# The last chunk's first MLP layer by 20 products of blocks in place of 22

## The chip, the cores and the metric

The kernel runs on one core of a Trainium2 chip. The metric is the device time of one launch in microseconds. All times below are of this kernel before the change: three timed runs, and one execution taken by the hardware profiler.

## What is computed

The reference has two stages. A recurrence (a delta rule) runs over 768 tokens for 4 batches of 8 heads of dimension 48; its output, 3072 tokens by 384, goes through an MLP with a SiLU:

```
for t in range(S):
    y[t]  = q[t] @ state
    v_old = k_n[t] @ state
    state = state + beta[t] * outer(k_n[t], v[t] - v_old)
x = y as (B*S, H*D)                 # 3072 x 384
h = x @ w_in                        # 384 x 2048
out = (h * sigmoid(h)) @ w_out      # 2048 x 384
```

All of it is in float32.

## The kernel before

**Chunks.** The 768 tokens are six chunks of 128 (c = 0 to 5, `NCH` = 6), and each chunk has two halves of 64 tokens (`hf`). The recurrence of chunk c (`solve(c)`, and the inversion of its triangular blocks beforehand, `invert`) is interleaved with the MLP of the chunk before it. A half's tokens of all four batches are 256 columns (`GT`); a chunk's inputs to the MLP are the two tiles `xTs[c, 0]` and `xTs[c, 1]`, each three blocks of 128 rows by 256 columns.

**One order per engine.** `pin` chains every compute instruction to the one before it on its engine, and `in_line` does so with the DMAs of SyncE. So the order in which the program calls things is the order in which each engine executes them. An instruction that waits holds up everything behind it on its engine.

**MLP in steps.** The MLP is a generator, `pieces`; `run(n)` advances it by n steps. The outer loop over c advances the recurrence by a stage (`go(solving)`) and the MLP by one or two steps in turn. For c = 5 there are eight such passes (n = 0 to 7), with these stages of the recurrence: the first merge (tile py, line 847; evacuated into y), the keys of the first half (ph, line 893; VectorE adds ph into vf, line 898), the second merge (px, line 847; into xi), the inner products and the old state's outputs of the first half (pz, line 905, and pyc, line 973), the update of the state with the new outputs (pu, line 925, with VectorE's addition to state at line 932; pyc, line 986), the copies of the outputs into xT, the keys of the second half (ph and vf again), and the inner products of the second half (pz and pyc again). Meanwhile the MLP steps are those of chunk 4's second layer. A last stage makes the outputs of the second half, and the rest of the MLP then runs to the end.

**First layer, chunks 2 to 5** (`hidden_by_products`, matmuls at line 1168). The weights w_in are three blocks of rows by pairs of column blocks; f counts 16 blocks of 128 columns, two to a pair. With the two halves of the tokens this makes small block products, of which linear combinations save some: 22 products for two units of two pairs each, instead of 24, on sums of weights (tile sums_of_w_in, made once) and sums of inputs (`sum_x`, five subtractions, line 1156). One product is `product(...)`: two matmuls of 128x128 weights by 256 columns into one PSUM bank. A chunk has 44 products in a list `items`; after some of them ScalarE copies the bank into gT (`by_act`, line 600), VectorE adds it to gT (line 1183), or ScalarE applies the Silu (lines 1189 and 1195). Banks of PSUM are handed out in turn: `hu` takes the two banks that the second layer's px and py had, `hx` two others.

**Second layer** (`combine(c, hf)`, matmuls at line 1334). For each half there are seven chains of eight matmuls of 192 columns, into px and py by turns; each chain is two MLP steps. In the middle of some chains VectorE makes sums of gT (`sum_g`, S1 to S4, line 1314) for later chains. Behind chains, ScalarE copies a bank into kept (line 1342), which frees it, and VectorE adds kept to o (line 1345); kept is one buffer. In the middle of the seventh chain of hf = 1 the kernel makes the next chunk's sums of inputs.

Of the kernel before, what the change touches and what calls it, by code (L numbers as in the profile page):

```python
# [10 lines left out]
FP32 = mybir.dt.float32  # L11
U32 = mybir.dt.uint32
ACTF = mybir.ActivationFunctionType
ALU = mybir.AluOpType
# [5 lines left out]
def kernel(  # L20
# [10 lines left out]
    nc = tc.nc  # L31
    B, H, S, D = q.shape
    DM, DFF = moe_w_in.shape
    P = 128
    C = P
    assert S % C == 0 and D == 48 and H == 8 and B == 4 and DM == H * D and DM == 3 * P
    NCH = S // C
# [5 lines left out]
    NKT = DM // P  # L43
    NFF = DFF // P
    HB = B // 2
    HH = HB * H
    GT = B * W
# [9 lines left out]
    banks = ctx.enter_context(tc.tile_pool(name="banks", bufs=1, space=PSUM))  # L57
# [5 lines left out]
    def bank(room, name):  # L63

        tag = room[0]
        room.rotate(-1)
        return pools.get(tag, banks).tile([P, 512], FP32, name=name, tag=tag)
# [12 lines left out]
    def pin(op):  # L80

        engine = op.ins.engine
        if engine in pins:
            behind(op, pins[engine])
        pins[engine] = op
        return op
# [19 lines left out]
    def go(steps, n=1):  # L106
        for _ in range(n):
            next(steps, None)
# [25 lines left out]
    spare_s = wS[:].rearrange("p k f t -> p (k f t)")  # L134
# [464 lines left out]
    def by_act(to, of):  # L599
        return pin(nc.scalar.copy(to, of))  # L600
# [496 lines left out]
    def home(c, hf):  # L1097

        return 1 - hf if c < 2 else hf
# [32 lines left out]
    def w_of(a, j):  # L1132
        return w_in[:, a].rearrange("p (f j t) -> p f j t", j=2, t=P)[:, :, j]
# [14 lines left out]
    def sum_x(c):  # L1148

        early, late = (xTs[c, hf] for hf in range(2))  # L1150
        for to, left, right in (
            (sums_of_x[:, 0], late[:, 0], early[:, 0]), (sums_of_x[:, 1], late[:, 1], sums_of_x[:, 0]),
            (late[:, 0], late[:, 1], late[:, 0]), (sums_of_x[:, 2], early[:, 1], sums_of_x[:, 1]),
            (sums_of_x[:, 3], early[:, 2], late[:, 2]),
        ):
            pin(nc.vector.tensor_tensor(out=to, in0=left, in1=right, op=ALU.subtract))

    def hidden_by_products(c):
# [68 lines left out]
        for n, (to, weights, moving, fs, start, after) in enumerate(items):  # L1227
# [8 lines left out]
                CC.append(rooms[1])  # L1236
            yield

    def store(c, hf, o, n, cols=slice(0, DM), two_queues=False):
        for u in range(HB):  # L1240
            row = (n * HB + u) * S + c * C + hf * W
            issue(out[row : row + W, cols], o[W * u : W * (u + 1), n, cols], two_queues and u == 1)
# [76 lines left out]
    def combine(c, hf):  # L1319

        o = mlp.tile([P, 2, DM], FP32, name="o", bufs=1)
        kept = mlp.tile([P, HM], FP32, name="kept", bufs=1)
        px, py = bank(M, "px"), bank(M, "py")
        left, right = slice(0, HM), slice(HM, DM)
        last = c == NCH - 1 and hf == 1
        order = list(range(NFF // 2)) if c < 2 else [2 * u + i for u in UNITS for i in range(2)]

        def chain(to, a, b, start=False):
            for n, f in enumerate(order):
                if isinstance(a, int):  # L1330
                    at = sums_of_g[:, a, f]
                else:
                    at = gT[:, home(c, hf), f, a[0] * GT + a[1] * C : a[0] * GT + (a[1] + 1) * C]
                pin(nc.tensor.matmul(  # L1334
                    to, lhsT=at, rhs=quarter(f, *b) if isinstance(b, tuple) else sums_of_w[b][:, f],
                    start=start and n == 0, stop=n == NFF // 2 - 1, skip_group_check=True,
                ))
                if n % 4 == 3:
                    yield

        def keep(of):
            pin(nc.scalar.mul(kept[:], of, 0.5))  # L1342

        def add(to, of):
            pin(nc.vector.tensor_tensor(out=to, in0=to, in1=of, op=ALU.add))  # L1345

        def steps(chain, *halfway):
            for n, _ in enumerate(chain):
                if n == 1:
                    break  # L1350
                for what in halfway:
                    if what is sum_x:
                        sum_x(c + 1)
                    else:
                        sum_g(c, *(what if len(what) == 3 else (hf, *what)))
                yield

        first, then, ahead, parts = (), (), (), PARTS
        if c < 2:
            first, parts = ((S1, NG - 1), (S2, NG - 1)), range(NG)  # L1360
        elif hf == 0:
            first, then = (tuple((which, fs) for fs in PARTS) for which in (S1, S2))
        else:
            first = tuple((S2, fs) for fs in PARTS)
        if hf == 1 and c + 1 < NCH:
            ahead = (sum_x,)
        elif hf == 0 and c > 1:
            ahead = tuple((1, S1, fs) for fs in PARTS)
        yield from steps(chain(px[:, left], (0, 0), (0, 0), True), *first)
        yield  # L1370
        yield from steps(chain(px[:, right], (1, 1), 2), *then)
        pin(nc.scalar.mul(o[:, :, left], px[:, 0:DM].rearrange("p (n m) -> p n m", n=2), 0.5))
        yield
        yield from steps(chain(py[:, left], 0, (0, 1), True))
        pin(nc.scalar.mul(o[:, 1, right], py[:, left], 0.5))
        yield
        yield from steps(chain(px[:, left], 1, 1), *((S3, g) for g in parts))
        pin(nc.scalar.mul(o[:, 0, right], px[:, left], 0.5))
        yield
        yield from steps(chain(py[:, right], (1, 0), (1, 0)), *((S4, g) for g in parts))  # L1380
        keep(py[:, right])
        add(o[:, 0, left], kept[:])
        if last:
            store(c, hf, o, 0, left)
        yield
        yield from steps(chain(px[:, left], 0, 0))
        keep(px[:, left])
        add(o[:, 1].rearrange("p (n m) -> p n m", n=2), kept[:].unsqueeze(1).to_broadcast([P, 2, HM]))
        if last:
            store(c, hf, o, 1)  # L1390
        yield
        yield from steps(chain(py[:, left], 1, (1, 1)), *ahead)
        if last:
            pin(nc.vector.scalar_tensor_tensor(
                out=o[:, 0, right], in0=py[:, left], scalar=0.5, in1=o[:, 0, right], op0=ALU.mult, op1=ALU.add
            ))
            store(c, hf, o, 0, right, True)
            yield
            return
        keep(py[:, left])  # L1400
        add(o[:, 0, right], kept[:])
        for n in range(2):
            store(c, hf, o, n)
        yield

    def feed_forward(c):

        if c > 1:
            yield from hidden_by_products(c)
        for hf in range(2):  # L1410
            if c == 1:
                yield from hidden(c, hf)
            yield from combine(c, hf)
# [209 lines left out]
    def run(n=1):  # L1623

        for _ in range(n):
            done[0] += 1
            name = next(needed, None)
            if name is not None:
                until(name)
            go(pieces)  # L1630
            begin_soon()
# [147 lines left out]
    def start(c):  # L1779

        return 2 * (NFF + OUTPUT) + (c - 2) * (ITEMS + 2 * OUTPUT)

    def run_to(at):

        assert done[0] <= at
        run(at - done[0])
# [40 lines left out]
    for c in range(2, NCH):  # L1827
        solving, more = solve(c), c + 1 < NCH
        for n in range(8):
            go(solving)  # L1830
            run((1, 1, 2, 2, 1, 1, 2, 2)[n] if c == 2 else (2, 2, 2, 2, 1, 1, 2, 2)[n])
            if n == 2 and c > 2 and more:
                assert done[0] >= start(c) - OUTPUT - 4
                load_blocks(k, c + 1, G1)
            if n == 3 and c > 2 and more:
                load_blocks(q, c + 1, G0)
            if n > 0:
                go(after, 8)
        go(after, 99)
        go(solving)  # L1840
        run()
        assert next(solving, 0) == 0
        if c == 2:
            pieces = chained(pieces, *(feed_forward(c) for c in range(2, NCH)))
        if not more:
            break
        run(1 if c == 2 else 2)
        step = block_steps(c + 1)
        ready = prepare(c + 1)
        go(ready)  # L1850
        run()
        go(ready)
        go(sums_in)
        go(sums_in)
        linked(load_v, c + 1)
        load_k(c + 2)
        run_to(start(c))
        paced(invert(c + 1, step), 7 if c == 2 else 4)
        after = lengths(c + 2) if c + 2 < NCH else iter(())
        run_to(start(c) + ITEMS + 3)  # L1860
        for g in range(2):
            size(c + 1, g)
        for n in range(3 if c == 2 else 2):
            go(after, 2 - n)
            run()
        go(after, 1)
# [31 lines left out]
```

## Time and profile before

| | |
|---|---|
| median of three runs | 630.88 us (628.24 to 633.61) |
| the profiled execution, its own time | 628.09 us |
| its span, first to last instruction | 626.3 us |
| mean granted clock of TensorE | 0.986 |
| busy: TensorE, VectorE, ScalarE, GpSimd | 610.0, 442.5, 244.4, 82.0 us |

The span is what the trace shows; the time of the execution has 1.8 us around it. A busy time is a sum over instructions of one engine; a row of a timeline gives the start, the length, the engine, the line, the operation, the tiles and the shapes, and in brackets how long the engine had been idle and what ended that. PE is TensorE's matmuls, PEld its weight loads, DVE VectorE, ACT ScalarE, POOL GpSimd.

### The profile page before, as it was taken

Reading aid. Unit: us, or ns where it says so; the run is one execution under the profiler, and the core shown is the slowest. Engines: PE = TensorE matmul, PEld = TensorE weight load, DVE = VectorE, ACT = ScalarE, POOL = GpSimd, SP = SyncE. Lnnn points to the kernel's source line nnn. Section 1 sums busy time; section 2 is a strip of 40 time slices with the busy share of each in tenths; the row PEclk is TensorE's granted clock in tenths of the full one; section 3 lists DMA queues with packets and bytes.
Section 4 is the critical chain, followed back from the end, with each engine's and each line's share of the span. In section 5 each row is a group of like instructions: output and inputs, shape, how many; then the busy total and the mean of one; then the engine's idle time right before and its main releaser. Section 6 shows DMA issues by size and latency. Waiting matters only on the chain.

```text
span 626.3 us, 21887 instructions
## 1 busy us (share of the span) xinstructions
PE 610.0 (97%) x9570; PEld 535.0 (85%) x9570; DVE 442.5 (71%) x946; ACT 244.4 (39%) x554; POOL 82.0 (13%) x83
## 2 busy tenths in 40 slices
PE   7889999999999999999999999999999999999997
PEld 5678788666789988898888998899998899988997
DVE  5855889998889975879977869976868944321332
ACT  3656655251351134443424433423533324434201
POOL 5443631246000010000010000010000010000000
PEclk9859999999999999999999999999999999999999
DMA  7754654164426571245073444084350051010011
GB/s 157 175 119 160 213 137 102 51 170 123 104 48 135 99 146 33 66 88 108 0 157 96 93 105 90 6 151 115 82 121 16 19 94 38 18 27 0 1 26 26
DMA packets 143935, 55.06 MB, mean 88 GB/s; under 512 B 113488, under 2 KB 137296, under 8 KB 143840
## 3 DMA queue, kind: packets, MB, share of 16 engines
q1 hardware_dynamic: 143360, 53.00, 37.8%
q8 instruction: 75, 1.23, 0.8%
q10 hardware_dynamic: 480, 0.67, 0.4%
q14 instruction: 20, 0.16, 0.1%
HBM read 40.99 MB, written 10.49 MB: 82 GB/s over the span
## 4 chain that ended last, share of the span: by engine, by line
PE 93%; DMA 2%; ACT 2%; issue 1%; DVE 1%; SPq 0%; DVEq 0%
PE px L1334 16%; PE phid L1114 13%; PE hu L1168 13%; PE py L1334 12%; PE hx L1168 11%; PE po L1257 7%; PE pa L585 4%; PE pz L905 3%; PE ph L893 2%; PE pyc L986 2%; PE pu L925 2%; PE pyc L973 2%; PE pt L556 1%; PE py L847 1%; PE px L847 1%
## 5 line engine op out<-in xcount | busy, mean ns | idle before, releaser
L1114 PE MATMUL phid<-xT,w_in 128*128 128x256 f32 x384 | 88.9, 385 | 0.0
L1114 PEld LDWEIGHTS phid<-xT,w_in 128*128 128x128 f32 x384 | 71.1, 190 | 10.0 <-issue 0.3
L1334 PE MATMUL py<-w_out,sums_of_g 128*128 128x192 f32 x320 | 57.4, 329 | 0.8 <-issue 0.8
L1334 PE MATMUL px<-sums_of_w,sums_of_g 128*128 128x192 f32 x320 | 57.2, 330 | 0.0
L1334 PEld LDWEIGHTS py<-w_out,sums_of_g 128*128 128x128 f32 x320 | 52.2, 190 | 1.5 <-issue 0.9
L1334 PEld LDWEIGHTS px<-sums_of_w,sums_of_g 128*128 128x128 f32 x320 | 52.1, 190 | 1.0 <-issue 0.5
L688 DVE SCALAR_TENSOR_TENSOR rank<-g,step,x 128x31 f32<-128x31 f32 (+15 forms) x124 | 49.6, 400 | 3.1
L1168 PE MATMUL hx<-xT,w_in 128*128 128x256 f32 x192 | 48.0, 379 | 0.0
L693 DVE TENSOR_TENSOR x<-x,rank 128x31 f32<-128x31 f32 (+15 forms) x124 | 42.5, 342 | 4.4
L1168 PE MATMUL hu<-xT,w_in 128*128 128x256 f32 x192 | 45.4, 379 | 0.0
L1183 DVE TENSOR_TENSOR gT<-gT,hx 128x512 f32<-128x512 f32 x32 | 21.9, 686 | 33.0 <-PE hx L1168 32.3
L1314 DVE TENSOR_TENSOR sums_of_g<-gT 128x512 f32<-128x512 f32 (+2 forms) x44 | 27.5, 662 | 22.6 <-PE py L1334 18.8
L1168 PEld LDWEIGHTS hu<-xT,w_in 128*128 128x128 f32 x192 | 36.5, 190 | 5.0
L1168 PEld LDWEIGHTS hx<-xT,w_in 128*128 128x128 f32 x192 | 36.4, 190 | 4.8
L521 POOL TENSOR_TENSOR vf<-vf,n_slot 128x768 f32<-128x768 f32 x10 | 14.6, 1476 | 189.8 <-DVE sums_of_g L1314 147.3
L1345 DVE TENSOR_TENSOR o<-o,kept 128x192 f32<-128x192 f32 (+1 forms) x29 | 12.4, 426 | 36.3 <-ACT kept L1342 36.3
L600 ACT COPY xT<-pyc 48x128 f32<-48x128 f32 (+2 forms) x120 | 31.2, 260 | 1.6
L600 ACT COPY gT<-hu 128x512 f32<-128x512 f32 x32 | 18.8, 586 | 30.6 <-PE hu L1168 30.6
L932 DVE TENSOR_TENSOR state<-state,pu 48x384 f32<-48x384 f32 x44 | 24.3, 552 | 8.5 <-PE pu L925 7.4
L1334 PE MATMUL px<-sums_of_w,gT 128*128 128x192 f32 x160 | 28.5, 329 | 0.6 <-issue 0.6
L1334 PE MATMUL py<-w_out,gT 128*128 128x192 f32 x160 | 29.0, 331 | 0.0
L1168 PE MATMUL hu<-sums_of_g,w_in 128*128 128x256 f32 x128 | 28.9, 379 | 0.0
(233 smaller groups left out, 1175.7 us busy)
## 6 DMA issues: line engine op xcount, KB each, us to landing
vf<-in_v_dram SPq DMA_DIRECT2D x48, 96.0 KB, 2.7
out_dram<-o SPq DMA_DIRECT2D x42, 96.0 KB, 2.3
w_out<-in_moe_w_in_dram SPq DMA_DIRECT2D x12, 256.0 KB, 3.5
sums_of_w<-in_moe_w_out_dram SPq DMA_DIRECT2D x8, 384.0 KB, 3.8
blocks<-ap SPq DMA_DIRECT2D x40, 64.0 KB, 2.1
g<-blocks SPq DMA_DIRECT2D x4, 512.0 KB, 3.7
up<-x SPq DMA_DIRECT2D x4, 512.0 KB, 3.1
xi<-up SPq DMA_DIRECT2D x16, 128.0 KB, 3.5
```

Source lines behind the costliest of these rows:

```text
L585: pin(nc.tensor.matmul(pa[e][half, p * n * W : (p + 1) * n * W], lhsT=kq[rows, p, 0, half], rhs=kq[rows, p, js[0] : js[-1] + 1, half], sta ...
L600: return pin(nc.scalar.copy(to, of))
L688: pin(nc.vector.scalar_tensor_tensor(out=tv, in0=g[:, 0:m, m : m + 1].to_broadcast([P, m, n]), scalar=step[:, m : m + 1], in1=x[:, m : m + ...
L693: yield pin(nc.vector.tensor_tensor(out=x[:, 0:m, m:T], in0=x[:, 0:m, m:T], in1=tv, op=ALU.add))
L905: yield pin(nc.tensor.matmul(pz[rows, n * D : (n + 1) * D], lhsT=xis[g][rows, u * H + 2 * p + e, :], rhs=vfs[c][rows, hf, g * HB + u, p, : ...
L932: pin(nc.vector.tensor_tensor(out=to, in0=to, in1=by_heads(pu[of]), op=ALU.add))
L1114: pin(nc.tensor.matmul(ph[:, j * GT : (j + 1) * GT], lhsT=w_in[:, a, (2 * f + j) * P : (2 * f + j + 1) * P], rhs=xTs[c, hf][:, a, :], star ...
L1168: pin(nc.tensor.matmul(to[:, GT * i : GT * (i + 1)], lhsT=weights[:, f], rhs=moving, start=start and i == 0, stop=True, skip_group_check=True,
L1183: return lambda: pin(nc.vector.tensor_tensor(out=at(fs, j, hf), in0=at(fs, j, hf), in1=of(room), op=ALU.add))
L1257: pin(nc.tensor.matmul(pos[i][:, 0:DM], lhsT=hidden_of(0, hf, f // 2)[:, at : at + C], rhs=w_outs[f // HFF][:, f % HFF, :], start=(f == 0) ...
L1314: pin(nc.vector.tensor_tensor(out=sums_of_g[:, k, fs], in0=of[0], in1=of[1], op=op))
L1334: pin(nc.tensor.matmul(to, lhsT=at, rhs=quarter(f, *b) if isinstance(b, tuple) else sums_of_w[b][:, f], start=start and n == 0, stop=n == ...
```

## The change

For the last chunk alone (`BY_CHAINS`), the first layer goes through `hidden_by_chains`: two sides of ten products, for two values of u, so 40 products in place of 44. `CHAINS` lists them as (weights, inputs, output block, sign). Each product goes on accumulating in its side's bank until its chain ends, and after every product the bank's content is evacuated into gT: by ScalarE's copy where the output block has nothing yet, otherwise by VectorE's addition or subtraction; a block that has all of its parts gets its Silu two products later. The four banks are used in rotation.

The sums of weights are made by 18 VectorE instructions on 128x512 elements (`sum_weights`): two that turn a difference back into the plain weights, in place in w_in, and sixteen of `W_SUMS`, which write over w_in, sums_of_w_in and a buffer of keys that is out of use. `go(weight_sums, 2)` puts two behind each of the eight passes of c = 5, and two after the last stage. The sums of inputs (`sum_inputs`, twelve instructions on 128x256 elements, into the tile kq) take the place of `sum_x`, and are made in the middle of the sixth chain instead of the seventh. In the last chunk's second layer the order of f within a chain and the order of the two parts of each sum of gT change.

```diff
@@ -1236,6 +1236,120 @@
                 CC.append(rooms[1])
             yield
 
+    BY_CHAINS = (NCH - 1,)
+    GROUPS = ((0, 1), (0, 0), (1, 1), (1, 0))
+    W_SUMS = (
+        (12, 4, 1, 3, -1), (3, 3, 1, 9, 1), (13, 4, -1, 3, 1), (14, 4, -1, 5, 1), (5, 5, 1, 8, -1), (4, 4, -1, 5, 1),
+        (15, 0, 1, 6, 1), (16, 4, -1, 15, -1), (17, 10, 1, 11, -1), (18, 2, -1, 17, -1), (19, 18, -1, 1, -1),
+        (15, 7, 1, 15, -1), (6, 6, -1, 7, 1), (1, 15, -1, 1, -1), (11, 13, 1, 11, -1), (11, 11, 1, 2, 1),
+    )
+    X_SUMS = (
+        (6, 2, 1, 4, 1), (7, 6, -1, 1, 1), (8, 1, -1, 0, -1), (9, 0, 1, 6, 1), (10, 1, 1, 3, 1), (11, 10, 1, 4, -1),
+        (12, 0, 1, 10, 1), (13, 12, 1, 2, 1), (14, 5, 1, 6, 1), (15, 5, 1, 4, 1), (16, 10, 1, 5, 1), (17, 14, 1, 3, 1),
+    )
+    CHAINS = (
+        (
+            ((12, 1, 3, -1), (13, 7, 7, 1), (9, 8, 6, -1), (3, 9, 2, 1)),
+            ((14, 4, 2, 1), (4, 11, 3, -1), (16, 10, 5, -1), (7, 13, 4, 1)),
+            ((8, 15, 5, 1), (5, 16, 3, 1)),
+        ),
+        (
+            ((2, 5, 1, 1), (18, 14, 7, 1), (17, 15, 6, -1), (19, 2, 0, -1)),
+            ((11, 6, 6, -1), (10, 17, 7, 1)),
+            ((0, 0, 0, 1), (15, 12, 4, -1), (6, 8, 5, 1), (1, 3, 1, -1)),
+        ),
+    )
+
+    def weights_at(slot):
+        if slot < 4 * NKT:
+            h, j = GROUPS[slot // NKT]
+            return w_in[:, slot % NKT].rearrange("p (r h j t) -> p r h j t", r=4, h=2, j=2)[:, :, h, j]
+        n, of = slot - 4 * NKT, spare_s
+        if n >= 6:
+            n, of = n - 6, kbufs[NCH % 2][:].rearrange("p g r -> p (g r)")
+        return of[:, n * 4 * P : (n + 1) * 4 * P].rearrange("p (r t) -> p r t", r=4)
+
+    def inputs_at(c, slot):
+        if slot < 2 * NKT:
+            return xTs[c, slot % 2][:, slot // 2]
+        n = slot - 2 * NKT
+        return turned_kq[:].rearrange("p b j a t -> p (b j a t)")[:, n * GT : (n + 1) * GT]
+
+    def linear(to, a, of_a, b, of_b):
+        if of_a < 0 and of_b < 0:
+            return pin(nc.vector.scalar_tensor_tensor(
+                out=to, in0=a, scalar=-1.0, in1=b, op0=ALU.mult, op1=ALU.subtract
+            ))
+        if of_a < 0:
+            a, b = b, a
+        return pin(nc.vector.tensor_tensor(out=to, in0=a, in1=b, op=ALU.add if of_a == of_b else ALU.subtract))
+
+    def sum_weights():
+        for i in range(2):
+            fs = slice(NFF // 4 * i, NFF // 4 * (i + 1))
+            to = w_of(0, 1)[:, fs]
+            yield linear(to, w_of(0, 0)[:, fs], 1, to, -1)
+        for to, a, of_a, b, of_b in W_SUMS:
+            yield linear(weights_at(to), weights_at(a), of_a, weights_at(b), of_b)
+
+    def sum_inputs(c):
+        for to, a, of_a, b, of_b in X_SUMS:
+            linear(inputs_at(c, to), inputs_at(c, a), of_a, inputs_at(c, b), of_b)
+
+    def hidden_by_chains(c):
+
+        rooms = [A.popleft(), CC.popleft()]
+        sides = [
+            [bank(M, "hu") for _ in range(2)],
+            [banks.tile([P, 512], FP32, name="hx", tag=tag) for tag in rooms],
+        ]
+        left, signs = {}, {}
+        for side in CHAINS:
+            for chain in side:
+                for *_, o, _ in chain:
+                    left[0, o] = left[1, o] = left.get((0, o), 0) + 1
+
+        def at(u, o):
+            h, j = GROUPS[o // 2]
+            return gT[:, home(c, o % 2), 4 * u + h : 4 * u + h + 3 : 2, GT * j : GT * (j + 1)]
+
+        def evacuate(u, o, sign, room):
+            to, of = at(u, o), room[:].rearrange("p (f t) -> p f t", f=2)
+            if (u, o) not in signs:
+                signs[u, o] = sign
+                by_act(to, of)
+            else:
+                same = sign == signs[u, o]
+                pin(nc.vector.tensor_tensor(out=to, in0=to, in1=of, op=ALU.add if same else ALU.subtract))
+            left[u, o] -= 1
+
+        def silu(u, o):
+            pin(nc.scalar.activation(out=at(u, o), in_=at(u, o), func=ACTF.Silu, scale=-0.5 * signs[u, o]))
+
+        orders = [[(n == 0, *one) for chain in side for n, one in enumerate(chain)] for side in CHAINS]
+        items = [(side, u, *orders[side][n]) for n in range(len(orders[0])) for side in range(2) for u in range(2)]
+        waiting, ready = None, deque()
+        for n, (side, u, start, w, x, o, sign) in enumerate(items):
+            to, weights, moving = sides[side][u], weights_at(w), inputs_at(c, x)
+            for i in range(2):
+                pin(nc.tensor.matmul(
+                    to[:, GT * i : GT * (i + 1)], lhsT=weights[:, 2 * u + i], rhs=moving,
+                    start=start and i == 0, stop=True, skip_group_check=True,
+                ))
+            last = n == len(items) - 1
+            for one in (waiting, (u, o, sign, to) if last else None):
+                if one:
+                    evacuate(*one)
+                    if not left[one[0:2]]:
+                        ready.append((n + 2, *one[0:2]))
+            waiting = (u, o, sign, to)
+            while ready and (last or ready[0][0] <= n):
+                silu(*ready.popleft()[1:])
+            if last:
+                A.append(rooms[0])
+                CC.append(rooms[1])
+            yield
+
     def store(c, hf, o, n, cols=slice(0, DM), two_queues=False):
         for u in range(HB):
             row = (n * HB + u) * S + c * C + hf * W
@@ -1323,7 +1437,10 @@
         px, py = bank(M, "px"), bank(M, "py")
         left, right = slice(0, HM), slice(HM, DM)
         last = c == NCH - 1 and hf == 1
-        order = list(range(NFF // 2)) if c < 2 else [2 * u + i for u in UNITS for i in range(2)]
+        by_chains = c in BY_CHAINS
+        order = list(range(NFF // 2))
+        if c > 1 and not by_chains:
+            order = [2 * u + i for u in UNITS for i in range(2)]
 
         def chain(to, a, b, start=False):
             for n, f in enumerate(order):
@@ -1349,23 +1466,25 @@
                 if n == 1:
                     break
                 for what in halfway:
-                    if what is sum_x:
-                        sum_x(c + 1)
+                    if what in (sum_x, sum_inputs):
+                        what(c + 1)
                     else:
                         sum_g(c, *(what if len(what) == 3 else (hf, *what)))
                 yield
 
-        first, then, ahead, parts = (), (), (), PARTS
+        first, then, sooner, ahead, parts = (), (), (), (), PARTS[::-1] if by_chains else PARTS
         if c < 2:
             first, parts = ((S1, NG - 1), (S2, NG - 1)), range(NG)
         elif hf == 0:
-            first, then = (tuple((which, fs) for fs in PARTS) for which in (S1, S2))
+            first, then = (tuple((which, fs) for fs in parts) for which in (S1, S2))
         else:
-            first = tuple((S2, fs) for fs in PARTS)
-        if hf == 1 and c + 1 < NCH:
+            first = tuple((S2, fs) for fs in parts)
+        if hf == 1 and c + 1 in BY_CHAINS:
+            sooner = (sum_inputs,)
+        elif hf == 1 and c + 1 < NCH:
             ahead = (sum_x,)
         elif hf == 0 and c > 1:
-            ahead = tuple((1, S1, fs) for fs in PARTS)
+            ahead = tuple((1, S1, fs) for fs in parts)
         yield from steps(chain(px[:, left], (0, 0), (0, 0), True), *first)
         yield
         yield from steps(chain(px[:, right], (1, 1), 2), *then)
@@ -1383,7 +1502,7 @@
         if last:
             store(c, hf, o, 0, left)
         yield
-        yield from steps(chain(px[:, left], 0, 0))
+        yield from steps(chain(px[:, left], 0, 0), *sooner)
         keep(px[:, left])
         add(o[:, 1].rearrange("p (n m) -> p n m", n=2), kept[:].unsqueeze(1).to_broadcast([P, 2, HM]))
         if last:
@@ -1405,7 +1524,9 @@
 
     def feed_forward(c):
 
-        if c > 1:
+        if c in BY_CHAINS:
+            yield from hidden_by_chains(c)
+        elif c > 1:
             yield from hidden_by_products(c)
         for hf in range(2):
             if c == 1:
@@ -1780,6 +1901,8 @@
 
         return 2 * (NFF + OUTPUT) + (c - 2) * (ITEMS + 2 * OUTPUT)
 
+    weight_sums = sum_weights()
+
     def run_to(at):
 
         assert done[0] <= at
@@ -1836,9 +1959,13 @@
                 load_blocks(q, c + 1, G0)
             if n > 0:
                 go(after, 8)
+            if c in BY_CHAINS:
+                go(weight_sums, 2)
         go(after, 99)
         go(solving)
         run()
+        if c in BY_CHAINS:
+            go(weight_sums, 99)
         assert next(solving, 0) == 0
         if c == 2:
             pieces = chained(pieces, *(feed_forward(c) for c in range(2, NCH)))
```

## The prediction, made before the change was run

> **What bounds the kernel now.** I read the page first, then the chain of work that ended last in order of time over the last 130 us, then the timelines of VectorE and ScalarE over the stretch in which the change puts new work.
>
> ```profile
> span 626.3 us, 21887 instructions
> ...
> PE 610.0 (97%) x9570; PEld 535.0 (85%) x9570; DVE 442.5 (71%) x946; ACT 244.4 (39%) x554; POOL 82.0 (13%) x83
> ...
> PE 93%; DMA 2%; ACT 2%; issue 1%; DVE 1%; SPq 0%; DVEq 0%
> ```
>
> TensorE is the bound: it is busy for 97% of the span and is 93% of the chain that ended last. From chunk 4's second layer on, the chain in order of time names TensorE without a gap (start, length, what):
>
> ```profile
> 526.72 1.08 PE ph L893 x64
> ...
> 530.60 0.18 PE pz L905
> ...
> 545.74 2.60 PE py L1334 x16
> 548.34 0.86 PE hx L1168 x4
> ...
> 582.87 3.45 PE hu L1168 x16
> 586.32 5.20 PE px L1334 x32
> ```
>
> So the last chunk's first layer runs from 548.34 to 586.32, and TensorE's queue, whose order is fixed by the program, has no idle time on either side. Whatever shortens that queue shortens the end one for one; whatever makes TensorE wait lengthens it one for one. The windows view of the product line alone gives the price of a matrix instruction (PE busy, PE loads busy, clock):
>
> ```profile
> 548.20:586.20 38.00, 38.00 (x176) 33.23 (x176) 1.00 0.05 11
> ```
>
> 176 instructions in 38.00 us are 0.216 us each. The code issues 44 products of two matmuls, 88, so a matmul is two instructions, and a product takes 0.864 us.
>
> **Part 1: 40 products for 44.** The two sides have ten products each for two values of u: 40 products, 160 instructions. Removed: 16 x 0.216 = 3.45 us, all of it on the path. Shapes stay (128x128 by 256 columns).
>
> **Part 2: evacuations during the products.** Every product is now followed by one of its own: 16 copies by ScalarE (the first for each u and output), 24 adds by VectorE and 16 Silus by ScalarE. Prices, from the groups of before in the same stretch (count, busy us, mean ns of one):
>
> ```profile
> L1183 DVE TENSOR_TENSOR gT<-gT,hx 128x512 f32<-128x512 f32 x8 | 5.5, 687 | 22.1 <-PE hx L1168 22.1
> L600 ACT COPY gT<-hu 128x512 f32<-128x512 f32 x8 | 4.7, 586 | 7.6 <-PE hu L1168 7.6
> ...
> L1189 ACT ACTIVATE gT<-gT 128x512 f32<-128x512 f32 x4 | 2.5, 632 | 0.0
> ```
>
> VectorE: 24 x 0.69 = 16.6 us; ScalarE: 16 x 0.59 + 16 x 0.63 = 19.5 us; both inside 34.6 us of products. A bank is written again four products later, so 3 x 0.864 = 2.6 us are there for an evacuation of 0.7. The longest run of VectorE adds has one add per product (0.69 in 0.864), so no backlog grows. I cost this at nothing; its cover is those 2.6 us. Behind the last product two adds and four sums (0.69 each) stand before the third chain of the output needs the sums: about 3.5 us under the 5.20 us of the row at 586.32. Free also; the new order of f in the last chunk's output changes no count.
>
> **Part 3: the 18 sums of weights, two behind each of the eight steps of chunk 5's recurrence, two after.** Nearest rows, by form:
>
> ```profile
> L1293 DVE TENSOR_TENSOR sums_of_w<-sums_of_w,w_out 128x768 f32<-128x768 f32 x2 | 2.5, 1266 | 0.0
> ...
> L688 DVE SCALAR_TENSOR_TENSOR rank<-g,step,x 128x256 f32<-128x256 f32 x4 | 1.9, 485 | 0.1
> ...
> L693 DVE TENSOR_TENSOR x<-x,rank 128x256 f32<-128x256 f32 x4 | 1.7, 424 | 0.1
> ...
> L1144 DVE TENSOR_TENSOR w_in<-w_in 128x512 f32<-128x512 f32 x2 | 1.3, 681 | 0.0
> ```
>
> L1144 is nearly the same instruction (128x512, strided w_in): 0.68 us. Two independent ones in a row overlap, as this timeline row shows (two take 1.29, so the second starts 0.61 after the first):
>
> ```profile
> 187.03 1.29 DVE L1144 TENSOR_TENSOR sums_of_w_in<-sums_of_w_in,w_in 128x512 f32<-128x512 f32 x2
> ```
>
> Low end: 0.61 each. Four sums read the one just ahead of them and lose the overlap (0.75), and four use the other instruction, which costs 0.06 more (485 against 424). Upper end: the dearest sum of weights, 1266 x 512/768 = 0.84. I take 0.69 in the mean, next to L1144. All 18 are 12.4 us of VectorE. They issue no DMA, and the change moves none; stores and xT's transfers only shift with what they wait for. Most lie in its gaps (PE, PE loads, DVE busy):
>
> ```profile
> 514.00:518.00 4.00, 4.00 (x130) 3.73 (x121) 1.73 (x3) 1.48 (x3) 0.00 (x0) 1.00 0.01 4
> 518.00:522.00 4.00, 4.00 (x111) 3.81 (x102) 0.74 (x2) 1.34 (x4) 0.00 (x0) 1.00 0.02 4
> ...
> 530.00:534.00 4.00, 4.00 (x141) 3.72 (x140) 0.00 (x0) 1.01 (x3) 0.00 (x0) 1.00 0.43 102
> 534.00:538.00 4.00, 4.00 (x83) 3.70 (x82) 0.03 (x1) 1.92 (x5) 0.00 (x0) 1.00 0.02 4
> ```
>
> The pairs behind steps 0 to 2 and 6 onwards go there and cost nothing; with that cover gone each would cost up to 1.4 us. The pairs behind steps 3, 4 and 5 do not. VectorE is strictly in order, and there stands:
>
> ```profile
> 521.26 0.56 DVE L1345 TENSOR_TENSOR o<-o,kept 128x384 f32<-128x384 f32 x1 [4.38 <-ACT kept L1342]
> 521.74 1.28 DVE L1314 TENSOR_TENSOR sums_of_g<-gT 128x512 f32<-128x512 f32 x2
> 523.08 2.30 DVE L932 TENSOR_TENSOR state<-state,pu 48x384 f32<-48x384 f32 x4
> 527.08 0.36 DVE L1345 TENSOR_TENSOR o<-o,kept 128x192 f32<-128x192 f32 x1 [1.70 <-ACT kept L1342]
> 527.36 1.29 DVE L1314 TENSOR_TENSOR sums_of_g<-sums_of_g,gT 128x512 f32<-128x512 f32 x2
> 528.67 1.02 DVE L898 TENSOR_TENSOR vf<-vf,ph 128x384 f32<-128x384 f32 x2
> ```
>
> The pair behind step 3 goes in front of the state additions, which end at 525.38 now and are read by ph at 526.72: a slack of 1.34 us against about 1.36. That costs nothing or a tenth. The pairs behind steps 4 and 5 go on either side of the sums at 527.36, thus four sums between the addition to o at 527.08 (which cannot be earlier: it waits for ScalarE's kept) and the vf additions. The first vf addition ends at 529.2 now; pz reads it at 530.60: slack 1.4 us. Four sums are 4 x 0.69 = 2.75 us, so pz waits 2.75 - 1.4 = 1.35 us, with everything behind it on TensorE; bounds 2.42 - 1.4 = 1.0 and 3.38 - 1.4 = 2.0. The wait at ph, if any, is contained in it, since vf's time is fixed by VectorE. Next late would be z and pyc behind pz; they shift along with TensorE's queue.
>
> **Part 4: 12 sums of inputs instead of 5, one chain earlier.** They come in front of the addition to o (546.14), whose end lets ScalarE overwrite kept and so free bank py:
>
> ```profile
> 543.60 0.36 DVE L1345 TENSOR_TENSOR o<-o,kept 128x192 f32<-128x192 f32 x1 [1.73 <-ACT kept L1342]
> 546.14 0.56 DVE L1345 TENSOR_TENSOR o<-o,kept 128x384 f32<-128x384 f32 x1 [2.18 <-ACT kept L1342]
> 546.61 0.42 DVE L1156 TENSOR_TENSOR sums_of_g<-xT 128x256 f32<-128x256 f32 x1
> 547.12 0.43 DVE L1156 TENSOR_TENSOR sums_of_g<-xT,sums_of_g 128x256 f32<-128x256 f32 x1
> 547.46 0.42 DVE L1156 TENSOR_TENSOR xT<-xT 128x256 f32<-128x256 f32 x1
> ```
> ```profile
> 548.37 0.33 ACT L1342 ACTIVATE kept<-py 128x192 f32<-128x192 f32 x1 [2.27 <-PE py L1334]
> ```
>
> A sum that reads the one before starts 0.51 later, another 0.34 later. Three of the first and nine of the second are 4.6 us from 543.9: the addition runs from 548.5 to 549.05, kept to 549.45. Before, bank py was needed by the fifth product; now by the second, at 548.34 + 0.86 = 549.20. A wait of 0.25 us; between 0 (all at 0.34) and 0.7 (all at 0.42).
>
> **Sum:** -3.45 + 1.35 + 0.25 = -1.85 us; bounds -3.45 + 1.0 = -2.45 and -3.45 + 2.0 + 0.7 = -0.75. The profiled execution took 628.09 us (span 626.3 and 1.8 around it), and would take 626.2. The runs shown have a median of 630.88, 2.8 above it, and spread from 628.24 to 633.61. Against that median I say 629.0, with bounds of the mechanism 628.4 to 630.1.
>
> **Rivals.**
> (a) The whole 3.45 us arrives: 627.4. It needs pz not to wait, thus four sums within 1.4 us, 0.35 each. For it: no wait of TensorE in this stretch of before. Against: L1144's 681 ns.
> (b) TensorE's clock falls at the new wait. It did in this trace:
>
> ```profile
> 31.61 0.93 PE L798 MATMUL pl<-sums_of_w 32*32 32x32 f32 x26 [1.38 <-issue]
> ```
> ```profile
> 19.00:20.00 1.00, 1.00 (x6) 0.57 0.80 242
> ...
> 22.00:23.00 1.00, 1.00 (x17) 0.73 1.32 208
> ...
> 32.00:33.00 1.00, 1.00 (x65) 0.89 0.12 24
> 33.00:34.00 1.00, 1.00 (x68) 0.50 0.94 183
> ...
> 46.00:47.00 1.00, 1.00 (x9) 0.78 0.72 256
> ```
>
> A second after a wait of 1.38 us, about as long as mine, TensorE is at half clock (columns: PE busy, clock), and stays so for some 13.7 us (32.8 to 46.4); an earlier fall lasts 3.4 (19.1 to 22.5). Against: there small matmuls and further waits surround it, here mostly dense ones do. From a wait of about 1.4 us with sparse work beside it, it decides: two short intervals, 6.8 us at half speed, cost 3.4 us, and the kernel is slower than before: -1.85 + 3.4 = +1.55, 632.4. The shorter fall alone (1.7) ends at 630.7.
> The Trainium skill ("TensorE: Matmul & The Clock Gate", Part 1) says that the clock halves only after an idle window of about 3.4 us; by that, 1.35 us would leave the clock whole, the sum would stay at -1.85, and rival (b) would fall away. The row at 31.61 disagrees, so the rival keeps a chance.
> (c) The evacuations hold the products up. The point is an add of over 0.864 us or a lag of 1.8 us. If all 40 products wait 0.1 us: +4.0, thus +2.15, 633.0. Against: 0.69, and no wait in before, where products also reuse a bank four later.
>
> **Numbers.** Forecast 0.64, (a) 0.12, (b) 0.16, (c) 0.08. The range, 626.0 to 632.4, takes in the bounds, (a), the short form of (b), and the spread of the runs. One per cent, 6.3 us, is about what a measurement of this kernel can tell from no change: no case gains that (3.45 at most, 0.03 for a lucky measurement), and slower by it needs the clock low for the long form and another wait (0.05); 0.92 within.
>
> **What would show it.** Right: 160 product instructions in about 34.6 us; a wait of 1.0 to 2.0 us in front of pz in chunk 5's second half, put down to VectorE's vf, clock 1.00 behind it; some 0.25 us before the second product. A span of 624 to 625 us. Wrong: no wait at pz (then a), PEclk below 1 near 533 (b), waits spread over the products (c), or sums of weights far from 0.68 us.

## The result and the profile after

Thirteen runs of the changed kernel have a median of 625.82 us (624.09 to 628.53), thirteen of the kernel before 628.33 us (626.86 to 633.61): a ratio of 0.9954, 95% interval 0.9932 to 0.9976, thus 2.9 us less, between 1.5 and 4.3 (the medians alone lie 2.5 apart). The profiled execution took 627.13 us.

The page of the changed kernel (span, busy time by engine, chain that ended last):

```profile
span 625.4 us, 21910 instructions
...
PE 607.6 (97%) x9554; PEld 532.3 (85%) x9554; DVE 464.5 (74%) x983; ACT 247.5 (40%) x562; POOL 82.2 (13%) x83
...
PE 53%; DVE 2%; DMA 1%; ACT 1%; issue 1%; SPq 0%; DVEq 0%; ACTq 0%
```

TensorE has 16 instructions less. Its share of the chain, 53% after 93%, misleads: behind the first wait of TensorE for another engine, the chain turns off into that engine, and it does not come back to all of TensorE's work. The places at which it turns off are what to look at. In order of time (start, length, what) the changed kernel has

```profile
506.20 1.22 PE py L847 x82
...
532.69 0.25 PE pz L905
...
551.46 1.13 PE hu L1335 x4
...
585.40 5.20 PE px L1451 x32
...
621.84 0.36 DVE o L1513
```

and the kernel before, at the first and the last of these places:

```profile
505.40 1.22 PE py L847 x82
...
622.76 0.36 DVE o L1394
```

Two executions do not reach chunk 5 at the same moment (505.40 and 506.20, with the same instructions ahead). So I measure from py L847 to the last chunk's second layer: 586.32 - 505.40 = 80.92 us before, 585.40 - 506.20 = 79.20 us after, 1.72 less. It divides so: py L847 to the second pz, 25.20 before and 26.49 after; from there to the end of the seventh chain, 17.74 and 17.81; the products from the seventh chain's end, 37.98 and 34.90. (The 0.07 us of the middle part turn up in the table below wherever pz waits 1.3 us for VectorE, and only there.) Behind them, both take 36.44 us to the last addition to o.

The first loss is the wait at pz. TensorE's timeline and VectorE's in front of it:

```profile
527.39 1.22 PE L893 MATMUL ph<-state,kq 48*64 48x48 f32 x64
...
532.69 0.25 PE L905 MATMUL pz<-vf,xi 64*64 64x48 f32 x1 [1.27 <-DVE vf L898]
```
```profile
525.13 2.30 DVE L932 TENSOR_TENSOR state<-state,pu 48x384 f32<-48x384 f32 x4
527.83 0.36 DVE L1462 TENSOR_TENSOR o<-o,kept 128x192 f32<-128x192 f32 x1 [0.39 <-ACT kept L1459]
528.10 0.69 DVE L1285 TENSOR_TENSOR sums_of_w_in<-w_in 128x512 f32<-128x512 f32 x1
528.82 0.69 DVE L1280 SCALAR_TENSOR_TENSOR sums_of_w_in<-w_in,sums_of_w_in 128x512 f32<-128x512 f32 x1
529.43 1.29 DVE L1428 TENSOR_TENSOR sums_of_g<-sums_of_g,gT 128x512 f32<-128x512 f32 x2
530.64 0.68 DVE L1285 TENSOR_TENSOR sums_of_w_in<-w_in 128x512 f32<-128x512 f32 x1
531.36 0.69 DVE L1280 SCALAR_TENSOR_TENSOR kb<-w_in,sums_of_w_in 128x512 f32<-128x512 f32 x1
532.08 1.02 DVE L898 TENSOR_TENSOR vf<-vf,ph 128x384 f32<-128x384 f32 x2
```

The four sums take 0.72, 0.61, 0.72 and 0.72 us to the next start, 2.77 in all. From the addition to o to vf are 4.25 us here (527.83 to 532.08) and 1.59 in the kernel before (527.08 to 528.67): vf comes 2.66 us later, pz had 1.4 us of slack, and the rest is its wait. The second loss is kept, which waits behind the twelve sums of inputs. VectorE's first sum and the addition behind the last, then ScalarE's timeline and TensorE's weight loads of the second product:

```profile
546.03 0.42 DVE L1285 TENSOR_TENSOR kq<-xT 128x256 f32<-128x256 f32 x1
...
550.43 0.55 DVE L1462 TENSOR_TENSOR o<-o,kept 128x384 f32<-128x384 f32 x1
```
```profile
551.08 0.33 ACT L1459 ACTIVATE kept<-py 128x192 f32<-128x192 f32 x1 [2.81 <-DVE o L1462]
```
```profile
551.46 0.73 PEld L1335 LDWEIGHTS hu<-xT,sums_of_w_in 128*128 128x128 f32 x4 [0.50 <-ACT kept L1459]
```

And the view of waits of the weight loads:

```profile
PEld pz L905 <- DVE vf L898: 1.6, 1, 1.6
PEld hu L1335 <- ACT kept L1459: 0.5, 1, 0.5
```

160 instructions at the 37.98/176 us of the kernel before would be 34.53 us; the products take 34.90. The windows around the wait at pz (length; busy time of PE, PE loads, VectorE, ScalarE and GpSimd; clock; the last two columns are the DMA's share and GB/s) show the clock whole:

```profile
530.00:534.00 4.00, 2.73 (x99) 2.43 (x101) 3.94 (x8) 0.11 (x1) 0.00 (x0) 1.00 0.44 103
534.00:538.00 4.00, 4.00 (x105) 3.72 (x98) 2.80 (x5) 1.39 (x4) 0.00 (x0) 1.00 0.02 4
```

### The profile page after: what moved, and what is told of

The parts are those of the page before. It is cut to its first block, busy times and chain, and to the rows that moved or that the text cites. A ratio compares the mean times of both kernels' runs of the same rounds, so it can differ in the third digit from the quotient of the medians.

```text
span 625.4 us, 21910 instructions
## 1 busy us (share of the span) xinstructions
PE 607.6 (97%) x9554; PEld 532.3 (85%) x9554; DVE 464.5 (74%) x983; ACT 247.5 (40%) x562; POOL 82.2 (13%) x83
## 4 chain that ended last, share of the span: by engine, by line
PE 53%; DVE 2%; DMA 1%; ACT 1%; issue 1%; SPq 0%; DVEq 0%; ACTq 0%
PE px L1451 12%; PE py L1451 10%; PE hu L1168 9%; PE hx L1168 8%; PE hx L1335 3%; PE hu L1335 3%; PE pa L585 2%; PE pz L905 1%; PE pyc L986 1%; PE pyc L973 1%; PE ph L893 1%; PE pu L925 1%; PE py L847 1%; DMA xe<-low 1%; PE px L847 1%
## 5 line engine op out<-in xcount | busy, mean ns | idle before, releaser
L1114 PE MATMUL phid<-xT,w_in 128*128 128x256 f32 x384 | 90.7, 390 | 0.0
L1168 PE MATMUL hx<-xT,w_in 128*128 128x256 f32 x144 | 36.0, 379 | 0.0
L600 ACT COPY gT<-hu 128x512 f32<-128x512 f32 x36 | 21.1, 586 | 32.9 <-PE hu L1168 22.9
L1168 PE MATMUL hu<-xT,w_in 128*128 128x256 f32 x144 | 34.0, 379 | 0.0
L1168 PEld LDWEIGHTS hu<-xT,w_in 128*128 128x128 f32 x144 | 27.4, 190 | 3.7
L1168 PEld LDWEIGHTS hx<-xT,w_in 128*128 128x128 f32 x144 | 27.3, 190 | 3.6
L905 PEld LDWEIGHTS pz<-vf,xi 64*64 64x64 f32 x768 | 25.2, 142 | 4.5 <-issue 2.6
L1122 ACT ACTIVATE gT<-phid 128x512 f32<-128x512 f32 x24 | 14.4, 598 | 36.3 <-PE phid L1114 35.7
```

The source lines that it names most:

```text
L905: yield pin(nc.tensor.matmul(pz[rows, n * D : (n + 1) * D], lhsT=xis[g][rows, u * H + 2 * p + e, :], rhs=vfs[c][rows, hf, g * HB + u, p, : ...
L1114: pin(nc.tensor.matmul(ph[:, j * GT : (j + 1) * GT], lhsT=w_in[:, a, (2 * f + j) * P : (2 * f + j + 1) * P], rhs=xTs[c, hf][:, a, :], star ...
L1122: pin(nc.scalar.activation(out=hidden_of(c, hf, f), in_=ph[:], func=ACTF.Silu, scale=0.5))
L1168: pin(nc.tensor.matmul(to[:, GT * i : GT * (i + 1)], lhsT=weights[:, f], rhs=moving, start=start and i == 0, stop=True, skip_group_check=True,
```

## The experiments

All times of a stretch below run from py L847 of chunk 5 to the last chunk's second layer, with its three parts as above, and come from one profiled execution of each. The two parts from pz on agree within 0.02 us between executions of one program; the part ahead of pz does not (25.20 and 25.82 for the kernel before). The ratios are to the kernel before, timed beside each run.

| run | to pz | to chain 7's end | products | stretch | ratio, 95% interval |
|---|---|---|---|---|---|
| before | 25.20 | 17.74 | 37.98 | 80.92 | |
| before again | 25.82 | 17.74 | 37.99 | 81.55 | 1.0002 (0.9975 to 1.0030) |
| changed | 26.49 | 17.81 | 34.90 | 79.20 | 0.9954 (0.9932 to 0.9976) |
| changed again | 26.47 | 17.81 | 34.90 | 79.18 | 0.9997 (0.9964 to 1.0030) |
| weight sums moved | 25.39 | 17.74 | 34.90 | 78.03 | 0.9953 (0.9935 to 0.9971) |
| hx first | 26.86 | 17.81 | 34.53 | 79.20 | 0.9959 (0.9936 to 0.9982) |
| both | 25.14 | 17.74 | 34.54 | 77.42 | 0.9947 (0.9928 to 0.9966) |
| weight sums moved, input sums later | 25.42 | 17.74 | 34.53 | 77.69 | 0.9919 (0.9887 to 0.9951) |
| the same again | 25.58 | 17.74 | 34.54 | 77.86 | 0.9941 (0.9917 to 0.9965) |
| four more sums | 30.20 | 20.19 | 34.89 | 85.28 | 1.0026 (0.9996 to 1.0056) |
| nine more sums | 33.36 | 19.31 | 34.90 | 87.57 | (one run) |

**The kernel before, against itself.** No edit.

> The kernel before, unchanged, against itself. Theory (the anchor): the three runs first shown were a high draw from a spread that the kernel has anyway; then the ratio is 1.000 within its interval, single runs lie 5 us or more apart, and the profile's distance from py L847 of chunk 5 to the last chunk's second layer is again 80.9 us (505.40 to 586.32), while the start of that stretch moves by about 1 us from profile to profile. Rival (the change gains ahead of this stretch too): the start of the stretch is the same in every execution of this kernel, and the spread of its times is under 2 us.

Twelve runs have a median of 630.71 us (626.78 to 634.22), 29 of the same kernel beside them 629.99 (627.31 to 636.46). The profiled execution took 634.22 us against 628.09 of the first profile, and py L847 starts at 510.95 instead of 505.40, where I expected a shift of about 1 us. The windows of the first 60 us (length, PE busy, clock, then the DMA's two columns), first of the profile before:

```profile
0.00:15.00 15.00, 11.69 (x318) 1.00 0.78 158
15.00:30.00 15.00, 13.84 (x411) 0.89 0.77 178
30.00:45.00 15.00, 11.24 (x403) 0.59 0.53 101
45.00:60.00 15.00, 14.64 (x318) 0.95 0.51 169
```

and then of the same program's second profile:

```profile
0.00:15.00 15.00, 11.83 (x314) 0.95 0.72 152
15.00:30.00 15.00, 14.55 (x254) 0.60 0.86 199
30.00:45.00 15.00, 10.85 (x470) 0.63 0.46 89
45.00:60.00 15.00, 14.62 (x370) 0.84 0.47 155
```

The shortfall of the clock is 15 x (0 + 0.11 + 0.41 + 0.05) = 8.6 us of full speed in the one and 15 x (0.05 + 0.40 + 0.37 + 0.16) = 14.7 in the other: 6.1 us for 5.55 of delay. So these two executions lie apart by how much the clock fell in the first 60 us, among small matmuls and waits. This program's single runs spread over 9 us. In the 80 of them that were timed beside the experiments, a longer time goes with a lower mean granted clock (correlation -0.80); where in a run the clock fell, only the profiled executions show. Of the theory, the spread and its source hold. That the first three runs were a high draw does not: the medians here are 630.71 and 629.99, so 630.88 is a usual value of this kernel, and the 628.33 of the thirteen runs beside the changed kernel is a low one. Nor was the stretch 80.9 again but 81.55, with 0.62 more ahead of pz, where the profile shows small gaps that nothing releases ("issue").

**The weight sums moved away from passes 3 to 5.**

```diff
-                go(weight_sums, 2)
+                go(weight_sums, (2, 2, 6, 0, 0, 0, 4, 2)[n])
```

> The changed kernel with the pairs of weight sums behind passes 3, 4 and 5 moved: four more behind pass 2, two more behind pass 6. Theory (VectorE's order holds up pz): the wait of 1.27 us at pz is gone, py L847 to the last second layer takes 77.9 us instead of 79.2, the time is 1.3 us under the changed kernel's, ratio to before about 0.993. Rival (pz would be late anyway, for xi, the old state's outputs or ScalarE): a wait of 0.8 us or more stays, put down to another producer, and the stretch stays above 78.7 us.

```profile
507.51 1.22 PE py L847 x82
...
532.90 0.18 PE pz L905
...
551.60 1.13 PE hu L1335 x4
...
585.54 5.20 PE px L1451 x32
```

pz comes 25.39 us after py L847, 0.2 from the kernel before, and the products still take 34.90: of the two losses, this one alone is gone, and TensorE has no wait at pz left. That the eighteen sums cost a wait of 1.3 us in one order and none in another shows that the place was the cost, not the sums. The stretch is 78.03 us, where I expected 77.9. The time is 0.9953 of before, where I expected about 0.993, which lies just below the interval (0.9935 to 0.9971): I had taken the 1.3 us off the changed kernel's first ratio, and that was a favourable one, as its repeat below shows.

**The hx banks first.**

```diff
-        items = [(side, u, *orders[side][n]) for n in range(len(orders[0])) for side in range(2) for u in range(2)]
+        items = [(side, u, *orders[side][n]) for n in range(len(orders[0])) for side in (1, 0) for u in range(2)]
```

> The changed kernel with the two hx banks' products ahead of the two hu banks' in every round, so that bank py is needed by the fourth product and not by the second. Theory (the twelve sums of inputs make kept late, and kept holds bank py): the wait in front of the second product is gone, 1.1 us of hu x4 shrinks to 0.86, and the stretch from py L847 to the last second layer takes 78.8 us instead of 79.2, with the wait of 1.27 us at pz still there. Rival (the products wait for the sums themselves): the same 0.4 us turns up in front of another product, and the stretch stays at 79.2.

The products take 34.53 us, 160 times the 37.98/176 of the kernel before, and no product waits: the cause was bank py. But the expected 78.8 us did not come. The part ahead of pz has 0.37 us more than in the changed kernel, which this edit does not touch. And half of the gain is given back behind the products; the chain, and the wait of the weight loads that goes with it:

```profile
586.50 5.39 PE px L1451 x32
```
```profile
PEld px L1451 <- DVE gT L1323: 0.3, 1, 0.3
```

Now hu's products are the last ones, and px, which takes hu's bank, waits 0.19 us for VectorE's addition from it.

**Both.**

> Both edits. Theory (the two waits are all that the change gave back): no wait of TensorE in this stretch, 160 product instructions in 34.5 us, py L847 to the last second layer in 77.5 us, 3.45 us under the kernel before; time some 1.7 us under the changed kernel's, ratio to before about 0.993. Rival (a third cost shows once these two are gone, evacuations or the clock): the stretch stays above 78 us, with waits spread over the products.

77.42 us, 3.50 under the kernel before, against 3.45 removed; the products take 34.54, with no wait in front of any, and the clock stays whole. There is no third cost inside the stretch. The chain behind it has 5.38 us, as in the run before.

**The input sums in the seventh chain, the weight sums moved, the banks in their old order.**

```diff
-            sooner = (sum_inputs,)
+            ahead = (sum_inputs,)
```

The edit of the weight sums above goes with it.

> The changed kernel with the weight sums moved as in the run before (four more behind pass 2, two more behind pass 6, none behind 3, 4 and 5), the banks in their old order, and the twelve sums of inputs in the middle of the seventh chain instead of the sixth. Theory (kept is late only because the sums of inputs stand in front of the addition to o; nothing but the second round of products reads a sum): no wait at pz, none in front of the second product, 34.53 us of products, and the first chain behind them in 5.20 us and not 5.38, so 77.3 to 77.5 us from py L847, 3.4 us under the kernel before, ratio about 0.994. Rival (the sums are then late for the second round of products): a wait of 0.2 to 1 us in front of the fifth or sixth product, and a stretch of 77.7 us or more.

```profile
550.69 1.73 PE hu L1335 x8
...
585.22 5.20 PE px L1451 x32
```

The products take 34.53 us with hu first, and the chain behind has its 5.20: this mends the second loss with nothing given back. The sums of inputs are in time for the second round. The stretch (77.69) is above the expected 77.5 because of the part ahead of pz again (25.42). No wait of TensorE's matmuls is left in the stretch or at the chain behind it, and the ratios are the lowest of all: 0.9919 here and 0.9941 when it was run again. Both intervals lie below 1; over the changed kernel it gains 1.5 us in the traces.

**Four more sums behind pass 4**, and **nine more**.

```diff
+                if n == 4:
+                    to, a, of_a, b, of_b = W_SUMS[6]
+                    for _ in range(4):
+                        linear(weights_at(to), weights_at(a), of_a, weights_at(b), of_b)
```

> The changed kernel with one of the weight sums (W_SUMS[6]) repeated four times behind pass 4, which changes no result and adds four VectorE instructions ahead of the vf additions. Theory (VectorE's queue alone sets pz): the wait at pz grows from 1.27 us by four starts of 0.61 to 0.72 us, to 3.7 to 4.2 us, py L847 to the last second layer from 79.2 to 81.6 to 82.1 us, and the kernel becomes slower than before by about 1 us in this stretch. Rival (b of the prediction, the clock falls at a wait in this place): on top of that the granted clock falls to 0.5 for 3.4 us or more within some 4 us of the wait, and the stretch takes 83.3 us or more.

> The same with nine repeats: a wait of 6.7 to 7.8 us. Theory (VectorE's queue alone): a stretch of 84.6 to 85.7 us at clock 1.00. Rival (the clock falls once a wait is long enough): the granted clock is 0.5 for at least 3.4 us, and the stretch takes 86.3 us or more. With the run of four repeats this puts the length at which the clock falls between two waits in the same place.

The waits at pz, with four more and then with nine:

```profile
PE pz L905 <- DVE vf L898: 4.2, 1, 4.2
```
```profile
PE pz L905 <- DVE vf L898: 7.8, 1, 7.8
```

That is (4.2 - 1.27)/4 = 0.73 and (7.8 - 1.27)/9 = 0.73 us for each added sum: VectorE's queue alone sets pz. And now the clock falls. Windows of 2 us of the run with four more (length, PE, PE loads, VectorE, ScalarE, GpSimd, clock, then the DMA's two columns):

```profile
532.00:534.00 2.00, 1.17 (x8) 0.87 (x6) 1.90 (x3) 0.00 (x0) 0.00 (x0) 1.00 0.32 73
534.00:536.00 2.00, 0.00 (x0) 0.00 (x0) 1.98 (x4) 0.00 (x0) 0.00 (x0) 0.94 0.53 126
536.00:538.00 2.00, 0.66 (x24) 0.66 (x28) 1.96 (x4) 0.00 (x0) 0.00 (x0) 0.50 0.02 4
...
542.00:544.00 2.00, 2.00 (x12) 2.00 (x12) 0.00 (x0) 0.49 (x1) 0.00 (x0) 0.86 0.00 0
```

and with nine more:

```profile
532.00:534.00 2.00, 1.99 (x13) 1.70 (x11) 1.90 (x4) 0.01 (x1) 0.00 (x0) 1.00 0.21 49
534.00:536.00 2.00, 0.00 (x0) 0.00 (x0) 1.90 (x4) 0.00 (x0) 0.00 (x0) 1.00 0.66 158
...
538.00:540.00 2.00, 0.00 (x0) 0.00 (x0) 2.00 (x4) 0.00 (x0) 0.00 (x0) 0.58 0.00 0
...
544.00:546.00 2.00, 2.00 (x60) 1.94 (x54) 1.90 (x4) 0.81 (x3) 0.00 (x0) 0.71 0.03 8
```

From the shares of these windows, TensorE is idle from 533.2, at half clock from 535.8 to 542.6 with four more; idle from 534.0, at half clock from 538.3 to 545.2 with nine. So it falls 2.6 and 4.3 us into the wait and stays down for 6.8 us both times. The price is in the second part of the table: 20.19 and 19.31 us instead of 17.8. (The first part also has 0.8 and 0.3 us more than the longer wait accounts for, which nothing here explains.) The run with nine pays less, as more of its low time passes while TensorE waits anyway. My theory, that the queue alone matters, falls for such waits: rival (b) of the prediction is a real mechanism, and 1.27 us did not set it off: all three profiles with that wait (changed, changed again, hx first) have the clock at 1.00 around it.

In time, the run with four more sums is 1.6 us over the kernel before (-0.3 to 3.5), where its stretch is 4.4 us over. That is outside the interval. The granted clocks of the timed runs may account for much of the gap, as an estimate: the ten runs have a mean of 0.9805, of which their fall in the stretch, 3.4 us of full speed in 632, takes 0.0054, so that 0.0141 was lost elsewhere; the sixteen runs of the kernel before have 0.9826 and lost 0.0174. The difference, 0.0033 of 632 us, is up to 2.1 us that the ten runs were spared elsewhere by chance. No run tests this.

**The changed kernel again, and the fastest version again.**

> The changed kernel, unedited, against the kernel before once more. In the traces the stretch that the change touches gains 1.7 us; the first comparison gave 2.9 us with an interval from 1.5 to 4.3. Theory (only the touched stretch gains, the rest is the spread of the first 60 us, where the clock falls now and then): the ratio lies near 0.9973, and the two intervals together come nearer to 1.7 us. Rival (something ahead of the stretch gains too): the ratio is again 0.9954 or less, and py L847 of chunk 5 starts earlier than in the kernel before at equal clock.

> The version without the two waits (sums moved, sums of inputs in the seventh chain) once more. Theory (only the touched stretch gains): 1.5 to 1.9 us under the changed kernel in this call and 3.2 to 3.5 us under the kernel before, ratio near 0.9947, with py L847 to the last second layer again at 77.3 to 77.7 us. Rival (the waits mattered less than the traces say): within 0.7 us of the changed kernel.

The changed kernel's ratio is 0.9997 in this repeat (0.9964 to 1.0030), the mean of the two 0.9976: 1.5 us, next to the 1.72 of the traces and away from the first 2.9. The stretch is 79.18 again, while the profiled execution reaches py L847 at 513.07 and took 634 us. I find no sign of a gain ahead of the stretch. The changed kernel's median is 3.0 us above its first one (628.84 after 625.82), and its runs have a mean granted clock of 0.9810 after 0.9861, which is 3.2 us of full speed. The version without the waits has 626.26 us beside 628.84, 2.6 less where I expected 1.5 to 1.9 and the traces have 1.3 to 1.5; its runs also had the better clock (mean 0.9848 beside 0.9810). Its ratio of 0.9941 (0.9917 to 0.9965) lies wholly below 1, and its interval holds the expected 0.9947. Its stretch, 77.86 us, is 0.16 above what I expected, again ahead of pz (25.58). How far it is ahead of the changed kernel, the traces say better than the times.

## Why the prediction was right and wrong

**What was wrong is the anchor.** The step that failed is "Against that median I say 629.0": the sum was put on the median of three runs, 630.88, and the range was reckoned from there, with a lower end of 626.0. In the runs beside the changed kernel the same program had a median of 628.33, 2.55 us lower, and the measured 625.82 missed the range by 0.2. What the prediction put at too little is how far a median of this kernel moves from one comparison to the next: 628.33 over 13 runs, then 629.99, 631.58 and 630.16. The three runs were not unusual among these; the first comparison was, in which both kernels were fast. The changed kernel's later median, 628.84, is 0.2 from the forecast 629.0. The spread of three runs that I had was 5.4 us, and I let it widen the range too little, above all downwards. Why the first comparison was fast is likely the clock (0.9861 for the changed kernel there, 0.9810 later), but for the kernel before in it only the profiled execution's clock (0.986) is on record, so this stays open.

The sum made against the profiled execution alone, 626.2, is 0.4 us from the measured 625.82. That is luck: the second profiled execution of the same program took 634.22. The changed kernel's span, 625.4, is a little over the 624 to 625 that the prediction named, as chunk 5 began 0.80 us later than in the profile before.

**The difference.** Forecast -1.85 us, with -2.45 to -0.75; in the traces -1.72 (-2.35 against the second profile of the kernel before, which has 0.62 more ahead of pz), in time -2.9 (-4.3 to -1.5) and then -0.2 (-2.3 to +1.9). So the mechanism and its size were right; each time alone is too coarse to tell. Term by term:

- *Products*: -3.45. The runs without waits have 34.53 and 34.54 us for the products, 37.98 less 3.45.
- *Evacuations at nothing*: right; no product waits for one, and rival (c) is out. The unmentioned cost, 0.19 us behind the products, exists only when hu's banks come last.
- *Weight sums*: 1.35 us at pz, measured 1.27 idle and 1.29 of shift. The four sums put vf off by 2.66 us, estimated 2.75. Both surcharges in the estimate were too dear: the other form of the instruction costs no 0.06 more at this size (0.69 both), and one that reads its predecessor starts 0.72 after it, not 0.75. The mean of 0.69 came out near because it was set next to L1144 and not made up of them. The state additions ended at 527.43, and ph had begun at 527.39 without a wait in the view of waits, as reckoned. Moving the pairs took the wait away.
- *Input sums*: 0.25 us, measured 0.37, and not made up as I had it. Kept was to end 1.11 us behind the start of the first product (549.45 less 548.34), and ended 0.91 behind it (551.41 less 550.50), since the twelve sums took 4.40 us and not 4.6; the first product takes 0.86, so kept itself was only 0.05 late. The other 0.32 us I had at nothing: I let the second product start as soon as kept had ended, but its weight load waits as well, starts at 551.46, and is not ahead of it any more.

**Rivals.** (a) is out: pz waits. (b) did not happen at 1.27 us, and happens at 4.2. The Trainium skill ("TensorE: Matmul & The Clock Gate", Part 1) has the clock halve after an idle window of about 3.4 us. By that, 1.27 us leaves it whole, and the trace agrees. The fall 2.6 us into a wait that follows dense matmuls is earlier than its figure; the return 6.8 us later is twice its window. The fall behind 1.38 us at the start of the kernel, on which my rival rested, stood among small matmuls and further waits; a wait of nearly that length behind dense ones did not bring it about.

**Left open:** why single parts ahead of pz differ by up to 0.6 us between executions of the same instructions, how long between 1.27 and 4.2 us the wait at pz has to be for the clock to fall, and what of the time with four more sums the estimate by the clock leaves over.

## What to carry to other kernels

Work that fills idle time of an engine is priced by what stands behind it in that engine's queue: the same eighteen instructions cost 1.3 us of the bound engine or nearly nothing, by where they were put. For each insertion, subtract the slack of the next thing that the bound engine reads from the inserted time; it gave 1.35 for 1.27 here. And make the sum against an anchor that is known as well as the difference: single runs of this kernel spread over 9 us, and its medians of 12 to 29 runs over 3.2, so no such median is an anchor for a change of 2. A forecast of the difference, held against the stretch in the traces, could be judged here; one of the time could not.

## What I had not expected of the hardware

A wait of 1.27 us behind dense matmuls left TensorE's clock whole; waits of 4.2 and 7.8 us in the same place halved it 2.6 and 4.3 us after they began, each time for 6.8 us. The falls at the start of the kernel that the prediction shows lasted 3.4 and 13.7 us: half of that and twice that. Executions of one program differ by 9 us (627.31 to 636.46); for two profiled ones, 5.55 us apart at the start of the stretch, the clock in the first 60 us accounts for it. Two VectorE instructions of 128x512 start 0.61 us apart, and 0.72 when the second reads what the first wrote.
